# Windowed attention into a two-pass feed-forward: seven ff tiles in the first pass, a margin on what TensorE waits for, and the first keys ahead of other loads

## The chip, the cores and the metric

The kernel runs on one core of a Trainium2 chip. The metric is the device time of one execution in microseconds (us). Before the change three executions took 1095.8, 1096.32 and 1097.32 us, so the median is 1096.32. Engines are called as the profile calls them: PE is TensorE (PEld its weight loads), DVE is VectorE, ACT is ScalarE, POOL is GpSimd and SP is SyncE, which issues every DMA here.

## The reference

Batch 8, 8 heads, 576 positions, head size 64. Each position attends to itself and the 127 before it, with a slope per head; the result, 4608 tokens of 512, goes through a feed-forward with 2048 inner columns.

```python
scores = scale * np.matmul(q, k.transpose(0, 1, 3, 2))
bias = slopes[:, None, None] * (-np.abs(rel).astype(np.float32))[None, :, :]
mask = (rel >= 0) & (rel < window)          # window = 128
scores = np.where(mask, scores + bias[None], -1000000000.0)
attn = softmax(scores)
x = (attn @ v).transpose(0, 2, 1, 3).reshape(4608, 512)
h = x @ w_in                                # 512 x 2048
sp = np.maximum(h, 0.0) + np.log1p(np.exp(-np.abs(h)))
out = (h * erf(sp)) @ w_out                 # 2048 x 512
```

## The kernel before

**Attention.** Two heads make a pair, so there are 32 pairs. A pair is worked in two spans: the first has three query tiles of 128 (score tiles 0, 1, 2), the second has two (3 and 4), which makes 160 score tiles. A score tile is a product on PE (line 520 for the first 16 spans, in plain fp32; line 531 for the rest, with k split into a high and a low part), the bias and row minimum on DVE (line 542), the exponential on ACT (line 552) and the division by the row sum on POOL (line 577). Then PE transposes the probabilities (line 595), DVE or ACT copies them out, and PE multiplies them with v (line 613). The first 16 spans are the "early" ones: the first spans of pairs 0 to 7, then their second spans. An early span loads q into a tile `a`, which POOL scales by a power of two for each head (line 455, with the table `head` of line 376), and k into a pair of tiles `kz`, whose other half of partitions POOL has cleared once (line 368). There are two such pairs of `kz` tiles, used in turn, and four `a` tiles. Later pairs load raw q and k (`qr`, `kr`), and DVE, ACT and POOL split them (lines 472 to 490).

**Feed-forward.** The 4608 tokens are 12 chunks of 384, the 2048 inner columns are 16 tiles of 128 ("ff tiles"). A unit is one chunk with one ff tile: a first group of 12 products (line 795, tile `h`), softplus and erf on ACT, a product, a high and a low part on DVE, ACT or POOL, and a second group of 9 products (line 855, tiles `o`). The first pass runs NF1 ff tiles over all chunks among the attention's work, as the chunks of x come out of it, and stores its partial sums (`pd`); the second pass runs the remaining ff tiles and adds the partial sums. Each weight tile arrives as 64-bit floating point words and is taken apart into a high and a low part (lines 684 to 704: one operation on ACT, five on DVE, a copy on any of three engines, and a last subtraction on DVE that gives `wli` or `wlo`). The weights of the second pass take over the attention's memory (`FIT` of them in each of two rows, the others where first-pass weights stood), so they are prepared after the attention has ended.

**What sets the order.** Every operation is put into a plan with a cost per engine, its buffers and a time `at`; `Plan.run` then walks through simulated time and gives each engine, whenever it is free, the ready operation with the lowest `at`. An operation counts as ready when the last of its inputs has ended plus a hop between the two engines (`hop`, line 140). A transfer is taken to need its bytes at 360 GB/s, one after another on a single line (line 278), plus two fixed times. The order found in this way is written out: on the chip each engine works through its list in that order and waits at whatever is not ready. PE fills gaps that the plan sees with products of a zero tile (`warm`, 40 of them, line 399). `step_time` gives score tiles their `at` (TE apart for the first NE tiles, TA after that), and TM is the spacing of the first pass's units, chosen so that all of them together span the same planned time for any NF1.

Of the kernel before, what the change touches and what calls it, by code (L numbers as in the profile page):

```python
# [8 lines left out]
F32 = mybir.dt.float32  # L9
# [8 lines left out]
B, H, S, D = 8, 8, 576, 64  # L18
NPAIR = H // 2
P = 128  # L20
WIN = 128
DM = H * D
# [4 lines left out]
NTT = CH // P  # L27
LOG_EXP_SET = "natural_log_exp_and_others"

NF1 = 6  # L30
FIT = 8
UPR = (4, 4)
TAIL = (2, 2)
EARLY = 16
# [5 lines left out]
PB, XB, OB, TB, TBB = 8, 3, 3, 2, 2  # L40
BT = 0

TE, NE = 2.3, 28
TA = 1.8
LL, LP, LT = 15, 6, 0
TM = 1.2 * TA * 20 / (1.5 * NF1)
# [85 lines left out]
class Plan:  # L132
# [7 lines left out]
    def hop(self, src, dst):  # L140
        if src == "PE":
            return 0.0 if "PE" in dst else 0.2
        return 0.2 if "Pool" in dst else 0.14

    def __init__(self):
        self.ops = []
# [36 lines left out]
    def run(self):  # L183
# [6 lines left out]
        transfer = 0.0  # L190
# [48 lines left out]
        while events:  # L239
            t = heapq.heappop(events)  # L240
            while events and events[0] <= t:
                heapq.heappop(events)
            while done and done[0][0] <= t + 1e-9:
                _, _, o = heapq.heappop(done)
                for b in o.bufs:
                    b.users -= 1
                    if b.users == 0 and b.tag is not None:
                        empty[key(b)].append(b.slot)
                for x in o.outs:
                    x.left -= 1  # L250
                    if not x.left:
                        late = max(
                            d.end + d.lag + (self.hop(d.engine, x.costs))
                            for d in x.deps
                        )
                        enable(x, max(late, t))
            for e in ("SP", "PE", "Act", "DVE", "Pool"):
                while free.get(e, 0.0) <= t + 1e-9 and ready.get(e):
                    best = None
                    for o in ready[e]:  # L260
                        if o.ready > t + self.WAIT[e] + 1e-9 or (best and (best.at, best.seq) < (o.at, o.seq)):
                            continue
                        if fits(o) and all(t + o.costs[e] <= max(free[x], t) + c for x, c in o.costs.items()):
                            best = o
                    if best is None or best.ready > t + 1e-9:
                        break
                    for x in best.costs:
                        ready[x].remove(best)
                    for b in best.bufs:
                        if b.tag is not None and id(b) not in placed:  # L270
                            placed.add(id(b))
                            b.slot = empty[key(b)].pop(0)
                            head[key(b)] += 1
                    best.engine, best.start = e, t
                    best.end = on_pe(best, t) if e == "PE" else t + best.costs[e]
                    free[e] = best.end
                    if best.moved:
                        transfer = max(transfer, best.end + 0.65) + best.moved / 360e3
                        best.lag = transfer + 0.9 - best.end
                    order.append(best)  # L280
                    heapq.heappush(done, (best.end + best.lag, best.seq, best))
                    heapq.heappush(events, best.end)
                    heapq.heappush(events, best.end + best.lag)
# [33 lines left out]
def dma(nbytes, n=1, us=0.475):  # L317
    return dict(costs={"SP": n * us}, moved=nbytes)
# [23 lines left out]
class Attention:  # L342


    def __init__(self, tc, plan, ctx, actx, qT, kT, vb, bias, ident, moe):
        self.nc, self.plan = tc.nc, plan
        self.qT, self.kT, self.vb = qT, kT, vb
        self.bias, self.ident, self.moe, self.spare = bias, ident, moe, (moe.ps_h, moe.ps_o)
        sb = lambda name: actx.enter_context(tc.tile_pool(name=name, bufs=1))
        ps = lambda name: ctx.enter_context(tc.tile_pool(name=name, bufs=1, space=PSUM))  # L350
        self.raw, self.split, self.pp, self.ptp, self.xsb = (
            sb(n) for n in ("raw", "split", "pp", "ptp", "xsb")
        )
        self.ps = ps("ps_a")
        vpool = sb("vpool")
        self.vbd = []
        for i in range(2):
            t = vpool.tile([P, 9, P], F32, tag=f"vbd{i}", name=f"vbd{i}")
            v = Buf(shape=[P, 9, P], ap=t)
            plan.op({"Pool": 1.2}, lambda e, t=t: self.nc.gpsimd.memset(t, 0.0), w=[v], at=-1)  # L360
            self.vbd.append(v)

        self.plain = []
        for i in range(2):
            pair = [Buf(self.split, [P, S], F32, f"kh{j}", 2, f"kz{i}_{j}") for j in range(2)]
            for j, k in enumerate(pair):
                zero = slice((1 - j) * D, (2 - j) * D)
                plan.op({"Pool": 0.6}, lambda e, k=k, zero=zero: self.nc.gpsimd.memset(k[zero, :], 0.0),
                        w=[k], at=-3)
            self.plain.append(pair)  # L370
        self.head = Buf(self.split, [P, NPAIR], F32, "head", 1, "head")

        def powers(e):
            for g in range(NPAIR):
                for j in range(2):
                    self.nc.gpsimd.memset(self.head[j * D : (j + 1) * D, g : g + 1], 2.0 ** (2 * g + j))

        plan.op({"Pool": 0.8}, powers, w=[self.head], at=-3)
        self.order = [(b, g) for b in range(B) for g in range(NPAIR)]
        self.step = self.loads = 0  # L380
        self.seq = 0
        self.warm_up()

        for w in range(2):
            for i in range(2 * NPAIR):
                self.span(i, w, self.operands(i, w), self.values(i, 4 * w, 6 + 3 * w))
        for i in range(2 * NPAIR, len(self.order)):
            operands, v = self.operands(i), self.values(i, 0, 9)
            for w in range(2):
                self.span(i, w, operands, v)  # L390
# [11 lines left out]
    def operands(self, i, w=None):  # L402

        nc, op = self.nc, self.plan.op
        sync = nc.sync.dma_start
        b, g = self.order[i]
        at = step_time(self.step) - LL
        q0, q1 = (0, S) if w is None else SPANS[w][1:3]
        k0 = max(0, q0 - WIN)
        nq, nk = q1 - q0, q1 - k0  # L410
        early = self.seq < EARLY
        nm = f"{i}_{w}"
        n = self.seq
        self.seq += 1
        if early:
            q = Buf(self.split, [P, S], F32, f"a{n % 2}", 2, "a" + nm)
            k = self.plain[n % 2]

            def both(e):
                for j in range(2):  # L420
                    rows = slice(j * D, (j + 1) * D)
                    sync(k[j][rows, :nk], self.kT[b, g, rows, k0:q1])

            op(emit=both, w=k, at=at, **dma(P * nk * 4, 2))
        else:
            q = Buf(self.raw, [P, S], F32, "qr", 1, "qr" + nm)
            k = Buf(self.raw, [P, 2, S], F32, "kr", 1, "kr" + nm)
            src = self.kT[b, g, :, k0:q1].rearrange("(j d) s -> d j s", j=2)

            def both(e):  # L430
                for half in range(2):
                    sync(k[half * D : (half + 1) * D, :, :nk], src)

            op(emit=both, w=[k], at=at, **dma(2 * P * nk * 4, 2, 0.65))
        op(emit=lambda e: sync(q[:, :nq], self.qT[b, g, :, q0:q1]), w=[q], at=at, **dma(P * nq * 4))
        at = step_time(self.step) - LP
        return (*(self.early_parts if early else self.parts)(nm, g, q, k, nq, nk, at), q0, k0)
# [222 lines left out]
class Weights:  # L660

    def __init__(self, nc, plan, place, stage, w_in, w_out, ffs):
        self.nc, self.plan, self.place, self.stage = nc, plan, place, stage
        self.src = (w_in, w_out)
        self.ffs = list(ffs)
        self.t = {}

    def prepare(self, which, f, at, after=()):  # L670
        nc, op = self.nc, self.plan.op
        nm = f"{'io'[which]}{f}"
        raw = Buf(self.stage, [P, DM, 2], I32, "wr", 2, f"wr{nm}")
# [1 line left out]
        t = Buf(self.stage, [P, DM], I32, "wt", 2, f"wt{nm}")  # L675
        op(emit=lambda e: nc.sync.dma_start(
            raw.all.rearrange("p n two -> p (n two)"), self.src[which][f].bitcast(I32)),
            w=[raw], at=at - 20, **dma(P * DM * 8))

        words = lambda k: raw[:, :, k]  # L680
        flt = lambda x: x.all.bitcast(F32)
# [204 lines left out]
def tile_kernel(ctx, tc, qT, kT, vb, w_in, w_out, bias, out, nb=B):  # L886
    nc = tc.nc
# [17 lines left out]
    stage = ctx.enter_context(tc.tile_pool(name="stage", bufs=1))  # L905
    moe = Moe(tc, plan, ctx, x_dram, part, out)
    actx = ctx.enter_context(ExitStack())
    Attention(tc, plan, ctx, actx, qT, kT, vb, bias_sb, ident, moe)
    ops = list(plan.ops)


    n1 = nch * NF1
    t0 = LEAD
    t1 = t0 + n1 * TM
    w1 = Weights(nc, plan, lambda k, f: (w1p, f"{k}_{f}"), stage, w_in, w_out, range(NF1))
    for k in range(2):
        for f in range(NF1):
            w1.prepare(k, f, t0 - W1A + (f * W1C + W1B * k) * TM)
# [60 lines left out]
```

## Time and profile before

| what | value |
| --- | --- |
| median of three executions | 1096.32 us |
| the profiled execution, its own time | 1095.57 us |
| its span, first to last instruction | 1093.8 us |
| outside the span (difference) | 1.8 us |
| mean granted clock of TensorE | 0.994 |
| first product that counts (line 520) starts | 6.72 us |
| first unit of the feed-forward (line 795) starts | 50.2 us |
| last product of the attention (line 613) starts | 502.7 us |

The tables by stretch give, for each engine, the time in which it was busy and the number of its instructions; PEclk is the share of TensorE's full clock that was granted. A wait is put down to the instruction whose end released it. An fp32 product shows as two instructions, so 40 `warm` products are 80 in the trace.

### The profile page before, as it was taken

To read this page: it belongs to the slowest core of one execution; us is meant where nothing else is said; L and a number is where in the kernel's file an instruction comes from. 1 tells how busy PE (TensorE), PEld (TensorE's weight loads), DVE (VectorE), ACT (ScalarE), POOL (GpSimd) and SP (SyncE) were. 2 spreads that over 40 slices of the span, in tenths; PEclk is the share of its full clock that TensorE was granted. 3 is DMA by queue.
4 is the path that set the end of the run, shared out by engine and by line. 5 is a ranking of instruction groups with operands and counts; after the bars stand their busy time and mean duration, and the time that the engine had idled before them with its cause. 6 is when DMAs were issued, how large, how long until landed. Compare 5 with 4: busy or idle time off the path is not lost.

```text
span 1093.8 us, 16894 instructions
## 1 busy us (share of the span) xinstructions
PE 1065.1 (97%) x6000; PEld 975.3 (89%) x6000; DVE 677.9 (62%) x1531; ACT 676.2 (62%) x1393; POOL 289.6 (26%) x438
## 2 busy tenths in 40 slices
PE   7998999999999989999999999999999999999998
PEld 7987889988999989899999998999999999999996
DVE  2789999878887787764888873433333334343342
ACT  4766887776777677765766663645535545445461
POOL 5645657565545555441100000000000000000000
PEclk9998999999999999999999999999999999999999
DMA  6553644646453453412434411220210210202102
GB/s 177 148 157 111 179 132 122 197 110 173 132 138 106 130 157 98 134 34 88 135 117 131 149 61 46 87 63 24 87 58 29 87 54 34 87 19 68 58 17 71
DMA packets 88260, 109.51 MB, mean 100 GB/s; under 512 B 45808, under 2 KB 58224, under 8 KB 88176
## 3 DMA queue, kind: packets, MB, share of 16 engines
q1 hardware_dynamic: 88176, 108.42, 33.6%
q8 instruction: 48, 0.79, 0.3%
q14 instruction: 36, 0.29, 0.1%
HBM read 80.08 MB, written 28.31 MB: 99 GB/s over the span
## 4 chain that ended last, share of the span: by engine, by line
PE 86%; DVE 5%; DMA 3%; POOL 3%; issue 1%; SPq 0%; ACT 0%; POOLq 0%; DVEq 0%
PE o L855 34%; PE h L795 34%; PE px L613 7%; PE t L595 5%; PE s L531 4%; POOL p L577 3%; PE s L520 2%; DMA xr<-xd 1%; DVE p L542 1%; DVE a_None L489 1%; DMA a<-q_t 1%; DMA kz<-k_t 1%; DMA wri<-w_in 1%; DVE hs L836 1%; DVE kl_None L486 0%
## 5 line engine op out<-in xcount | busy, mean ns | idle before, releaser
L795 PE MATMUL h<-xh,whi 128*128 128x384 f32 x768 | 263.9, 344 | 0.7 <-DVE xh L781 0.5
L795 PE MATMUL h<-xh,wli 128*128 128x384 f32 x768 | 260.0, 339 | 0.5 <-DVE wli L704 0.5
L795 PE MATMUL h<-xl,whi 128*128 128x384 f32 x768 | 259.1, 337 | 0.9 <-DVE xl L770 0.9
L855 PE MATMUL o<-who,gh 128*128 128x512 f32 x576 | 228.1, 396 | 0.0
L855 PE MATMUL o<-who,gl 128*128 128x512 f32 x576 | 227.5, 395 | 0.0
L855 PE MATMUL o<-wlo,gh 128*128 128x512 f32 x576 | 227.1, 394 | 0.0
L577 POOL TENSOR_SCALAR p<-p,st 128x256 f32<-128x256 f32 (+2 forms) x320 | 197.3, 635 | 95.2 <-DVE st L570 94.2
L777 ACT COPY hs<-h 128x384 f32<-128x384 f32 x113 | 53.8, 477 | 233.7 <-PE h L795 233.2
L552 ACT ACTIVATE p<-p,st 128x256 f32<-128x256 f32 (+2 forms) x320 | 149.0, 468 | 33.4 <-DVE st L542 32.9
L781 DVE COPY hs<-h 128x384 f32<-128x384 f32 x79 | 43.8, 555 | 192.6 <-PE h L795 192.4
L795 PEld LDWEIGHTS h<-xh,whi 128*128 128x128 f32 x768 | 145.4, 189 | 8.6 <-DVE xh L781 0.9
L795 PEld LDWEIGHTS h<-xl,whi 128*128 128x128 f32 x768 | 145.3, 189 | 7.5 <-DVE xl L770 1.1
L795 PEld LDWEIGHTS h<-xh,wli 128*128 128x128 f32 x768 | 144.8, 189 | 1.0 <-DVE wli L704 1.0
L542 DVE CUSTOM_DVE_ANT_0 p<-s,bias_sb 128x256 f32<-128x256 f32 (+2 forms) x320 | 108.8, 378 | 40.4 <-PE s L531 16.1
L855 PEld LDWEIGHTS o<-who,gl 128*128 128x128 f32 x576 | 108.0, 188 | 23.3
L855 PEld LDWEIGHTS o<-wlo,gh 128*128 128x128 f32 x576 | 108.3, 188 | 16.1
L855 PEld LDWEIGHTS o<-who,gh 128*128 128x128 f32 x576 | 108.4, 188 | 15.4
L836 DVE TENSOR_TENSOR hs<-s,hs 128x768 f32<-128x768 f32 x96 | 90.9, 970 | 23.6 <-ACT s L826 23.5
L840 DVE TENSOR_TENSOR gl<-hs,gh 128x768 fp32r<-128x768 f32 x96 | 90.8, 963 | 0.7 <-ACT gh L777 0.6
L595 PE MATMUL t<-ident,p 128*128 128x128 f32 x544 | 82.1, 276 | 6.6 <-POOL p L577 6.2
L595 PEld LDWEIGHTS t<-ident,p 128*128 128x128 f32 x544 | 64.6, 143 | 17.1 <-POOL p L577 9.8
L826 ACT ACTIVATE s<-s 128x768 f32<-128x768 f32 x96 | 76.0, 839 | 0.6
(78 smaller groups left out, 1486.3 us busy)
## 6 DMA issues: line engine op xcount, KB each, us to landing
xr<-xd SPq DMA_DIRECT2D x22, 768.0 KB, 4.3
kr_None<-k_t SPq DMA_DIRECT2D x48, 288.0 KB, 4.3
pd<-ot SPq DMA_DIRECT2D x36, 256.0 KB, 3.6
ot<-pd SPq DMA_DIRECT2D x36, 256.0 KB, 3.0
wri<-w_in SPq DMA_DIRECT2D x16, 512.0 KB, 4.3
wro<-w_out SPq DMA_DIRECT2D x16, 512.0 KB, 3.7
out_dram<-ot SPq DMA_DIRECT2D x32, 256.0 KB, 2.1
qr_None<-q_t SPq DMA_DIRECT2D x24, 288.0 KB, 4.3
```

The costliest lines, as they stand in the source:

```text
L542: nc.vector.tensor_tensor_reduce(out=pt[:m, c0:c1, j, :], in0=blocks(ps[:m, j, :n]), in1=blocks(self.bias[:m, c0 * 64 : c1 * 64]), scale=- ...
L552: nc.scalar.activation(dst, dst, AF.Exp, bias=low[:m, j : j + 1], scale=-1.0, accum_out=total[:m, j : j + 1],)
L577: nc.gpsimd.tensor_scalar(dst, dst, totals[t][:m, j : j + 1], 1.0, op0=ALU.mult, op1=ALU.mult)
L595: nc.tensor.matmul(ps[:, col : col + P], lhsT=p[t][:, kb].rearrange("p j d -> p (j d)"), rhs=self.ident[:, :], is_transpose=True, start=no ...
L613: self.nc.tensor.matmul(dst[:, q0 - base : q1 - base], lhsT=v[:, blk], rhs=sb[sbi][:, off : off + q1 - q0], start=(blk == order[0][0]), st ...
L777: self.nc.scalar.copy(out, src)
L781: self.nc.vector.tensor_copy(out, src)
L795: nc.tensor.matmul(ps[:, :CH], lhsT=ww[:, cs], rhs=xx[:, k], start=(k2 + k + n == 0), stop=(k2 + k + n == 4),)
L826: A.activation(s[:, :n], s[:, :n], AF.Erf)
L836: op({"DVE": dve(n2)}, lambda e, s=s, hs=hs, n=n: V.tensor_tensor(hs[:, :n], s[:, :n], hs[:, :n], ALU.mult), r=[s, hs], w=[hs], at=at)
L840: op({"DVE": dve(n2)}, lambda e, gh=gh, gl=gl, hs=hs, n=n: V.tensor_tensor(gl[:, :n], hs[:, :n], gh[:, :n], SUB), r=[hs, gh], w=[gl], at=at)
L855: nc.tensor.matmul(po.all, lhsT=g[:, j, cs], rhs=w.all, start=(u["start"] and n == 0), stop=(u["end"] and n == 2),)
```

## The change

NF1 goes from 6 to 7 and FIT from 8 to 7: the first pass has 84 units instead of 72, the second 108 instead of 120. TM follows, so units of the first pass are planned closer together. TE goes from 2.3 to 2.0 (the first 28 score tiles are planned earlier). The planner's hop into a PE operation from any other engine, DMAs included, grows by 0.6 us, and its transfer rate falls from 360 to 250 GB/s; both only alter the order. There are four pairs of `kz` tiles instead of two (the new ones in buffers of the low k parts, `kl`), so POOL clears eight tiles. And the loads of raw k (`kr`) and of weights (`wri`) gain dependences on early k loads, so that a load of raw k waits for the early k load four before the latest one, and a first-pass weight load for the fourth k load.

```diff
-NF1 = 6
-FIT = 8
+NF1 = 7
+FIT = 7
...
-TE, NE = 2.3, 28
+TE, NE = 2.0, 28
...
-        return 0.2 if "Pool" in dst else 0.14
+        return 0.2 if "Pool" in dst else 0.14 + 0.6 * ("PE" in dst)
...
-                        transfer = max(transfer, best.end + 0.65) + best.moved / 360e3
+                        transfer = max(transfer, best.end + 0.65) + best.moved / 250e3
...
-        for i in range(2):
-            pair = [Buf(self.split, [P, S], F32, f"kh{j}", 2, f"kz{i}_{j}") for j in range(2)]
+        for i in range(4):
+            pair = [Buf(self.split, [P, S], F32, f"k{'hl'[i // 2]}{j}", 2, f"kz{i}_{j}") for j in range(2)]
...
+        self.loaded = []
...
-            k = self.plain[n % 2]
+            k = self.plain[n % 4]
...
             op(emit=both, w=k, at=at, **dma(P * nk * 4, 2))
+            self.loaded.append(Buf(ap=True))
+            self.loaded[-1].writer = self.plan.ops[-1]
...
-            op(emit=both, w=[k], at=at, **dma(2 * P * nk * 4, 2, 0.65))
+            op(emit=both, r=self.loaded[-4:-3], w=[k], at=at, **dma(2 * P * nk * 4, 2, 0.65))
...
-            w=[raw], at=at - 20, **dma(P * DM * 8))
+            r=self.later, w=[raw], at=at - 20, **dma(P * DM * 8))
...
-    w1 = Weights(nc, plan, lambda k, f: (w1p, f"{k}_{f}"), stage, w_in, w_out, range(NF1))
+    w1 = Weights(nc, plan, lambda k, f: (w1p, f"{k}_{f}"), stage, w_in, w_out, range(NF1), attention.loaded[3:4])
```

What this does to the order shows best at three places. The first is SP's list of transfers at the very start; in the names the number behind `a` or `kz` is the early span's or the tile pair's number, `vbd` is v, `wri` is a weight tile, `kr8` and `qr8` belong to the first later pair. Before:

```order
L422 DMA kz0_0_166<-k_t 64x384
L422 DMA kz0_1_172<-k_t 64x384
L435 DMA a3_0_186<-q_t 128x384
L422 DMA kz1_0_177<-k_t 64x384
L422 DMA kz1_1_183<-k_t 64x384
L676 DMA wri0_205<-w_in 128x1024
L676 DMA wri1_209<-w_in 128x1024
L448 DMA vbd0_160<-v_b 64x6x64 x2
L432 DMA kr8_None_230<-k_t 64x2x576 x2
L448 DMA vbd1_161<-v_b 64x6x64 x2
L422 DMA kz0_0_166<-k_t 64x384
L422 DMA kz0_1_172<-k_t 64x384
```

Now, at the same place of SP's list:

```order
L439 DMA a3_0_185<-q_t 128x384
L423 DMA kz1_0_176<-k_t 64x384
L423 DMA kz1_1_181<-k_t 64x384
L423 DMA kz2_0_187<-k_t 64x384
L423 DMA kz2_1_192<-k_t 64x384
L439 DMA qr8_None_205<-q_t 128x576
L423 DMA kz3_0_196<-k_t 64x384
L423 DMA kz3_1_201<-k_t 64x384
L452 DMA vbd0_160<-v_b 64x6x64 x2
L452 DMA vbd1_161<-v_b 64x6x64 x2
L681 DMA wri0_257<-w_in 128x1024
L439 DMA a4_0_263<-q_t 128x384
```

The third pair's k stood behind two weight tiles, v and raw k; now it follows the second pair's at once, in tiles of its own, and the weights come after v.

The second place is the start of POOL's list and of PE's list. On POOL `head` is the table of scales and `a0` the first q; before:

```order
L368 MEMSET kz0_0_166 64x576
L368 MEMSET kz0_1_172 64x576
L368 MEMSET kz1_0_177 64x576
L368 MEMSET kz1_1_183 64x576
L376 MEMSET head_188 64x1 x8
L360 MEMSET vbd0_160 128x1152
L455 TENSOR_SCALAR a0_0_162<-a0_0_162,head_188 128x384
```

Now four more clears stand ahead of the first scaling of q:

```order
L368 MEMSET kz1_1_181 64x576
L368 MEMSET kz2_0_187 64x576
L368 MEMSET kz2_1_192 64x576
L368 MEMSET kz3_0_196 64x576
L368 MEMSET kz3_1_201 64x576
L376 MEMSET head_207 64x1 x8
L360 MEMSET vbd0_160 128x1152
L459 TENSOR_SCALAR a0_0_162<-a0_0_162,head_207 128x384
```

Everything that POOL does at the start moves back by these four rows. On PE, `s3` are score tiles of the fourth pair and `t0` is the first transpose; before:

```order
L520 MATMUL s3_0_324<-kz1_0_177,a3_0_186 128x128
L520 MATMUL s3_0_324<-kz1_1_183,a3_0_186 128x128
L520 MATMUL s3_1_333<-kz1_0_177,a3_0_186 128x256
L520 MATMUL s3_1_333<-kz1_1_183,a3_0_186 128x256
L399 MATMUL warm_ps_168<-warm_164 128x128 x2
L595 MATMUL t0_0_0_343<-ident_62,p0_0_226 128x128
```

Now, at the same eleven score tiles into the program:

```order
L524 MATMUL s3_0_323<-kz3_0_196,a3_0_185 128x128
L524 MATMUL s3_0_323<-kz3_1_201,a3_0_185 128x128
L400 MATMUL warm_ps_174<-warm_164 128x128 x2
L524 MATMUL s3_1_332<-kz3_0_196,a3_0_185 128x256
L524 MATMUL s3_1_332<-kz3_1_201,a3_0_185 128x256
L400 MATMUL warm_ps_174<-warm_164 128x128 x14
L599 MATMUL t0_0_0_365<-ident_62,p0_0_244 128x128
```

Fourteen zero products now stand between the last of these score tiles and the first transpose. The twelve that stood between the second and the third pair's scores are gone from there, and 22 instead of 17 precede the first score.

The third place is DVE's list around pair 10 (score tiles 51 to 55), where the first pass's last weights are finished: `p10_0` is the pair's first score tile, `wlo5` and `wlo6` are the sixth and seventh weight tile of w_out. Before, the twelfth and last tile is done ahead of the pair's first score:

```order
L781 CAST who5_1928<-wto5_1844 128x512
L489 TENSOR_TENSOR a11_None_0_1896<-qr11_None_1813,a11_None_0_1896 64x576
L704 TENSOR_TENSOR wlo5_1946<-wto5_1844,who5_1928 128x512
L570 RECIPROCAL st9_1_1848<-st9_1_1848 128x4
L542 ISA p10_0_1958,st10_0_1959<-s10_0_1930,bias_sb_63 128x2x64
```

Now the fourteenth is done behind the pair's fourth score tile:

```order
L697 SCALAR_TENSOR_TENSOR wqo6_1975<-wro6_1774,wqo6_1975 128x512
L841 TENSOR_TENSOR hs8_1590<-s8_1898,hs8_1590 128x768
L705 TENSOR_TENSOR wto6_1995<-wto6_1995,wqo6_1975 128x512
L574 RECIPROCAL st10_0_1887<-st10_0_1887 128x6
L546 ISA p10_3_2061,st10_1_2062<-s10_3_2034,bias_sb_63 128x4x64
...
L709 TENSOR_TENSOR wlo6_2079<-wto6_1995,who6_2065 128x512
L845 TENSOR_TENSOR gl8_2088<-hs8_1590,gh8_2051 128x768
```

So DVE has two more weight tiles within about the same score tiles.

More of the change, by code (lines that the diff above doesn't have):

```diff
@@ L660, with __init__ @@
 class Weights:
-    def __init__(self, nc, plan, place, stage, w_in, w_out, ffs):
+    def __init__(self, nc, plan, place, stage, w_in, w_out, ffs, later=()):
         self.nc, self.plan, self.place, self.stage = nc, plan, place, stage
         self.src = (w_in, w_out)
+        self.later = later
         self.ffs = list(ffs)
@@ L907, in tile_kernel @@
     actx = ctx.enter_context(ExitStack())
-    Attention(tc, plan, ctx, actx, qT, kT, vb, bias_sb, ident, moe)
+    attention = Attention(tc, plan, ctx, actx, qT, kT, vb, bias_sb, ident, moe)
     ops = list(plan.ops)
```

## The prediction

> **What bounds the kernel now.** I read the page's totals first, then a table by stretch, PE's waits, and the timeline of the start.
>
> ```profile
> span 1093.8 us, 16894 instructions
> PE 1065.1 (97%) x6000; PEld 975.3 (89%) x6000; DVE 677.9 (62%) x1531; ACT 676.2 (62%) x1393; POOL 289.6 (26%) x438
> ```
>
> PE is busy 97% of the span, and the change removes no product: it only moves units between the passes. So the gain can come only from time in which PE stands still, works on zero products, or has half its clock. The profiled execution took 1095.57 us, 1.8 more than its span and 0.75 less than the median 1096.32; I add changes to the span and keep those two offsets.
>
> I cut the span where score tiles 1, 9, 25, 33, 49, 57 and 81 and the end of the attention's products stand (four score instructions a tile, counted along the timeline: the 96 up to 49.5 are 24 tiles).
>
> ```profile
> 6.70:49.50 42.80, 20.82 (x96) 16.50 (x97) 0.96 0.61 165
> ```
>
> ```profile
> core 0: us, PE busy (x) PEld busy (x) DVE busy (x) ACT busy (x) POOL busy (x), PEclk, DMA share, GB/s
> 0.00:6.70 6.70, 5.65 (x34) 5.65 (x35) 0.17 (x1) 1.28 (x1) 5.60 (x21) 1.00 0.63 177
> 6.70:21.30 14.60, 9.93 (x59) 9.00 (x58) 4.65 (x29) 6.76 (x30) 5.50 (x11) 0.90 0.86 222
> 21.30:49.50 28.20, 28.20 (x193) 26.82 (x192) 20.03 (x84) 19.37 (x72) 17.05 (x35) 0.99 0.49 135
> 49.50:80.50 31.00, 29.08 (x192) 27.42 (x191) 23.90 (x74) 19.86 (x67) 17.27 (x31) 1.00 0.59 157
> 80.50:147.30 66.80, 60.46 (x359) 54.78 (x357) 62.67 (x152) 51.74 (x117) 36.99 (x46) 0.95 0.46 135
> 147.30:171.60 24.30, 22.89 (x143) 20.74 (x142) 21.84 (x58) 20.86 (x56) 14.57 (x17) 1.00 0.59 157
> 171.60:241.70 70.10, 68.66 (x457) 63.79 (x456) 61.22 (x172) 50.92 (x153) 46.70 (x67) 1.00 0.49 138
> 241.70:502.70 261.00, 253.82 (x1644) 236.82 (x1641) 194.98 (x553) 186.59 (x508) 133.89 (x201) 0.99 0.44 122
> 502.70:1093.80 591.10, 586.44 (x2937) 530.29 (x2936) 288.49 (x412) 318.87 (x392) 11.97 (x12) 1.00 0.22 71
> ```
>
> Three regimes show. At the start PE waits for loads. From 80.5 to 147.3 DVE is busy 62.67 of 66.8 us (94%): there DVE sets the pace. After 171.6 PE has short waits on other engines until the attention ends; after 502.7 it has none but the 5 us of the last stores, so nothing is to be had there.
>
> ```profile
> PE t L595 <- POOL p L577: 6.2, 10, 1.3
> PE s L531 <- DVE st L542: 4.8, 2, 2.8
> PE s L520 <- DMA kz<-k_t: 4.7, 1, 4.7
> PE s L520 <- DVE st L542: 3.4, 3, 1.8
> ```
>
> The longest single wait, 4.7 us, is for the third pair's k; the others are for probabilities from POOL and score buffers from DVE.
>
> **The change part by part. The start.** These are rows of PE, SP, POOL and DVE there:
>
> ```profile
> 6.72 4.51 PE L520 MATMUL s<-kz,a 128*128 128x128 f32 x24
> 11.07 2.84 PE L399 MATMUL warm_ps<-warm 128*128 128x128 f32 x24
> 18.58 5.32 PE L520 MATMUL s<-kz,a 128*128 128x128 f32 x20 [4.67 <-DMA kz<-k_t]
> 24.18 1.26 PE L595 MATMUL t<-ident,p 128*128 128x128 f32 x10
> 11.90 3.33 SPq L422 DMA_DIRECT2D kz<-k_t  x2
> 1.36 2.40 POOL L368 MEMSET kz<- 64x576 f32 x4
> 5.81 0.60 POOL L455 TENSOR_SCALAR a<-a,head 128x384 f32<-128x384 f32 x1
> 12.24 2.53 POOL L577 TENSOR_SCALAR p<-p,st 128x128 f32<-128x128 f32 x6 [3.15 <-DVE st L570]
> 11.96 0.18 DVE L570 RECIPROCAL st<-st 128x6 f32<-128x6 f32 x1
> ```
>
> The third pair's k is issued at 11.90, behind 1 MB of weights, v and raw k, and PE takes it at 18.58: between 11.07 and 18.58 lie 7.5 us without useful work. With its own tiles and its place behind the second pair this load no longer ends last. What is late next is POOL: four more clears at 2.40/4 = 0.6 us move the first scaled q from 5.81 to 8.2, done at 8.8, so the first score starts at about 9.1 instead of 6.72, a loss of 2.4. Then DVE: it took six tiles 5.24 us after the first score (11.96 - 6.72), so at 14.3; two more of the third pair at about 0.7 each and a reciprocal bring 15.9, which frees the score buffer for the eleventh tile, on PE until 16.8. Then 14 zero products (28 instructions; 24 took 2.84) end at 20.1, and the first transpose follows, if POOL has divided the first pair: reciprocal at about 15, the scaling of `a4` (0.6) and 2.53 us give 18.2. That leaves 1.9 us for the load of `a4`, which now waits behind a weight tile on SP, and which POOL meets ahead of those divisions. So the transpose comes at 20.1 instead of 24.18, with the same eleven score tiles done: **-4**. Bounds: -7.5 if the whole hole closed, +2.4 if only POOL's clears told. I take the worked-out value, near the middle. Both lists then run on with PE full in the row 21.30:49.50. The first weight tile comes later than before, but ACT meets it only ahead of the copies behind that transpose, so a wait for it is hidden until 20.1.
>
> **The DVE stretch.** In both orders all first-pass weights are done by about score tile 57, but there are 14 instead of 12. One tile costs DVE the six rows
>
> ```profile
> L689 DVE SCALAR_TENSOR_TENSOR wto<-wqo,wto 128x512 int32<-128x512 int32 x5 | 4.1, 829 | 0.0
> L700 DVE TENSOR_TENSOR wto<-wto,wqo 128x512 f32<-128x512 f32 x5 | 3.9, 779 | 0.0
> L704 DVE TENSOR_TENSOR wlo<-wto,who 128x512 fp32r<-128x512 f32 x5 | 3.9, 777 | 0.3 <-POOL who L779 0.2
> L692 DVE SCALAR_TENSOR_TENSOR wqo<-wro,wqo 128x512 f32<-128x512 uint32 x5 | 3.8, 765 | 0.0
> L687 DVE TENSOR_SCALAR wto<-wqo 128x512 int32<-128x512 int32 x5 | 3.0, 592 | 0.0
> L691 DVE TENSOR_SCALAR wqo<-wto 128x512 int32<-128x512 int32 x5 | 2.8, 560 | 0.0
> ```
>
> or 4.3 us together, two tiles 8.6. Other work leaves DVE for ACT: DVE's list up to score tile 57, each row at its line's mean, grows by 4.4, of which 2.3 stand before tile 25, where DVE has room (rows 6.70 to 49.50: 24.68 of 42.8 busy). That leaves 2.1. PE is not the bound here, and what it does meanwhile is less: up to score tile 57 its list held 17 first and 8 second groups of units, now 16.5 and 6.7. The groups cost
>
> ```profile
> 512.08 2.10 PE h L795 x12
> 510.00 2.08 PE o L855 x9
> ```
>
> so 0.5 x 2.10 + 1.3 x 2.08 = 3.8 us of units are put off to where PE is the bound. The stretch costs **+5.9**. Bounds: 0 if the rest of DVE's idle time takes it in and PE meets no more waits; 8.6 + 3.8 = 12.4 if no work leaves DVE. I take the count, as the order shows what leaves.
>
> **After 171.6 us.** PE's idle time there is 70.10 - 68.66 and 261.00 - 253.82, together 8.6 us, and a clock of 0.99 costs up to 2.6. From score tile 57 to the last attention product PE now has 43.5 first and 45.6 second groups between the score tiles instead of 38 and 40.7: 5.5 x 2.10 + 4.9 x 2.08 = 21.7 us more to do while the others deliver. With the hop longer by 0.6 the planner also sets PE's readers later behind their writers. The upper bound of the gain is 21.7: the attention ends when it did, with all of this done beside it. The lower is 0: PE ends the attention 21.7 later and waits as before. I take the visible idle time and half of the clock's share: **-10**. Where the edit is free: the copying of chunks, softplus tables (three rounds more with a third table load) and partial sums run on ACT, busy 237.52 of 331.1 there; if that cover went, one round costs the load of a table.
>
> ```profile
> 171.60:502.70 331.10, 322.48 (x2097) 300.61 (x2096) 256.19 (x724) 237.52 (x660) 180.59 (x268) 0.99 0.45 126
> ```
>
> The second pass's weights come no later against PE: 24 first groups of the first pass stand behind the attention's last product instead of 17, and there are 18 tiles to prepare instead of 20.
>
> Would a margin of 0.6 do? Two late waits tell:
>
> ```profile
> 395.17 1.76 DVE L489 TENSOR_TENSOR a_None<-qr_None,a_None 64x576 fp32r<-64x576 f32 x1
> 383.91 0.75 DVE L489 TENSOR_TENSOR a_None<-qr_None,a_None 64x576 fp32r<-64x576 f32 x1
> 447.11 7.62 DMA xr<-xd
> ```
>
> The first ran 1.0 us over its usual 0.75 with POOL's divisions beside it, and PE stood 2.8 us; the second is a load whose 768 KB the planner put at 2.2 us of transfer (now 3.1) and which took 7.62 in all. Both exceed 0.6, so the margin alone wouldn't have covered them; the added units have to. [...]
>
> **Sum:** -4 + 5.9 - 10 = -8, a profiled run of 1087.5 and a median of **1088**.
>
> **Rivals.**
> - *The attention keeps its own pace.* The put-off units cost nothing since all later idle time takes them: -4 and about -15 after 171.6, near 1077. For it: from 241.70 to 502.70 no other engine is busy over 75%. Against: DVE is at 87% from 171.60 to 241.70, and the visible 8.6 is less than 15. It covers 1070 to 1082.
> - *Waits longer than the margin stay.* POOL and DVE deliver late by 1 us and more, as shown; the late gain is only what the start and the DVE stretch take back: -4 + 5.9 - 2 = 0, so 1096. The changed rates then reorder the lists and do nothing else.
> - *Slower: DVE is the bound up to the first pass's last weights.* All 8.6 us of the two tiles tell, 3.8 of units are put off, and PE, waiting more between 80 and 170, loses clock again as in the row 80.50:147.30 (0.05 of 66.8 is 3.3): -4 + 8.6 + 3.8 + 3.3 - 6 = +6, so 1102. It decides where the seventh `wlo` ends later than PE's list needs it, that is where DVE's share between score tiles 33 and 57 rises above 94%.
>
> **How the numbers follow.** My forecast (1082 to 1094) gets 0.47, the first rival 0.25, no change 0.13, slower 0.15. A measurement can tell 0.2%, 2.2 us, from no change. Faster is then 0.72, same 0.13, slower 0.15. The range of 8 in 10 reaches from the start and the late gain at 18 with nothing lost between, 1074, to 1100, inside the slower rival.
>
> **What would show it.** Right: the first score near 9.1, no wait for `kz` after it, the first transpose near 20; DVE over 90% busy between score tiles 33 and 57 with PE's clock below 1; PE's idle time behind score tile 57 under 4 us; the attention's last product near 509 (502.7 - 4 + 2.1 - 10, plus 21.7 - 3.8 of units done before it). Wrong: POOL waiting on `a4` ahead of its divisions beyond 18 us, a first unit later than 50 us, or PE waiting for second-pass weights behind the attention.

## The result and the profile after

| what | before | changed |
| --- | --- | --- |
| median, same chip, four executions each | 1096.82 us | 1084.67 us |
| ratio to before, 95% interval | 1 | 0.9882 [0.9866, 0.9897] |
| the profiled execution, its own time | 1095.57 us | 1082.40 us |
| span | 1093.8 us | 1080.6 us |
| PE not busy (span less PE's busy time) | 28.7 us | 17.3 us |
| first score starts | 6.72 us | 8.90 us |
| first unit of the feed-forward | 50.18 us | 47.52 us |
| last product of the attention | 502.69 us | 507.50 us |

The kernel became faster by 12 us, where 8 were forecast. (One execution each of e4, e6 and e10 below took 1757 to 6005 us and is left out; as it is the one that e4's profile shows, the same kernel was run again as e10.) The totals of the changed kernel's page show where to look:

```profile
span 1080.6 us, 16860 instructions
...
PE 1063.3 (98%) x6000; PEld 975.9 (90%) x6000; DVE 678.3 (63%) x1535; ACT 682.0 (63%) x1398; POOL 293.5 (27%) x436
```

PE's busy time fell by 1.8 us only (1065.1 to 1063.3); the time in which it was not busy fell by 11.4. The table by stretch says when. It is cut at score tiles 1, 25, 33, 57, 81 and the attention's last product, which now stand elsewhere; columns as in the prediction's table.

```profile
0.00:8.90 8.90, 7.51 (x44) 7.32 (x44) 0.17 (x1) 1.28 (x1) 7.65 (x25) 1.00 0.63 183
8.90:46.84 37.94, 37.55 (x252) 34.99 (x253) 28.50 (x120) 27.16 (x106) 24.86 (x47) 1.00 0.62 168
46.84:73.50 26.66, 26.21 (x173) 25.10 (x171) 23.37 (x70) 16.36 (x55) 16.85 (x29) 1.00 0.69 189
73.50:165.60 92.10, 82.94 (x493) 75.60 (x492) 84.71 (x214) 71.10 (x181) 52.73 (x64) 0.94 0.52 143
165.60:237.20 71.60, 70.65 (x462) 65.53 (x461) 61.88 (x173) 55.83 (x156) 46.05 (x66) 1.00 0.53 149
237.20:507.50 270.30, 269.91 (x1744) 253.61 (x1742) 198.70 (x560) 199.72 (x521) 134.29 (x200) 1.00 0.41 114
507.50:1080.60 573.10, 568.57 (x2844) 513.71 (x2843) 281.00 (x401) 310.58 (x380) 11.06 (x9) 1.00 0.22 73
```

From score tile 57 to the attention's end PE now stands still for 0.95 + 0.39 = 1.3 us, where it was 8.6. Between tiles 33 and 57 it still does for 9.2 us, at a clock of 0.94: more than half of the 17.3 us that are left is there. PE's waits, grouped by what they were for (total, number, longest), agree:

```profile
PE t L599 <- POOL p L581: 5.7, 4, 3.0
PE o L860 <- DVE wlo L709: 1.3, 2, 1.0
...
PE s L535 <- DVE st L546: 0.7, 2, 0.4
```

The wait of 4.7 us for the third pair's k is gone, and the score buffers (`st`) cost 0.7 instead of 4.8 and 3.4. The timeline of PE at the start:

```profile
1.05 7.51 PE L400 MATMUL warm_ps<-warm 128*128 128x128 f32 x44 [1.05 <-DVE warm L398]
8.90 5.06 PE L524 MATMUL s<-kz,a 128*128 128x128 f32 x28 [0.34 <-POOL a L459]
13.80 0.61 PE L400 MATMUL warm_ps<-warm 128*128 128x128 f32 x4
14.24 2.34 PE L524 MATMUL s<-kz,a 128*128 128x256 f32 x12
16.42 0.61 PE L400 MATMUL warm_ps<-warm 128*128 128x128 f32 x4
16.86 1.03 PE L524 MATMUL s<-kz,a 128*128 128x256 f32 x4
17.73 3.29 PE L400 MATMUL warm_ps<-warm 128*128 128x128 f32 x28
20.86 1.25 PE L599 MATMUL t<-ident,p 128*128 128x128 f32 x10
```

The first score waits for the q that POOL scales (8.90 instead of 6.72), eleven score tiles follow without a stop, and the first transpose comes at 20.86 instead of 24.18.

### The profile page after: what moved, and what is told of

It reads as the page before. It is cut to its first block, busy times and chain, and to the rows that moved or that the text cites. A ratio compares the mean times of both kernels' runs of the same rounds, so it can differ in the third digit from the quotient of the medians.

```text
span 1080.6 us, 16860 instructions
## 1 busy us (share of the span) xinstructions
PE 1063.3 (98%) x6000; PEld 975.9 (90%) x6000; DVE 678.3 (63%) x1535; ACT 682.0 (63%) x1398; POOL 293.5 (27%) x436
## 4 chain that ended last, share of the span: by engine, by line
PE 94%; POOL 3%; ACT 1%; DVE 1%; issue 1%; POOLq 0%
PE h L800 36%; PE o L860 36%; PE px L617 8%; PE t L599 6%; PE s L535 5%; PE s L524 2%; POOL p L581 1%; ACT p L556 0%; POOL kz L368 0%; PE warm_ps L400 0%; POOL kh_None L480 0%; ACT pa L499 0%; POOL a_None L480 0%; DVE p L546 0%; ACT s L829 0%
## 5 line engine op out<-in xcount | busy, mean ns | idle before, releaser
L581 POOL TENSOR_SCALAR p<-p,st 128x256 f32<-128x256 f32 (+2 forms) x320 | 201.4, 647 | 86.5 <-DVE st L574 83.1
L784 POOL TENSOR_SCALAR gh<-hs 128x768 fp32r<-128x768 f32 x18 | 20.8, 1157 | 375.5 <-DVE hs L841 375.4
L841 DVE TENSOR_TENSOR hs<-s,hs 128x768 f32<-128x768 f32 x96 | 89.7, 958 | 20.2 <-ACT s L831 20.2
L845 DVE TENSOR_TENSOR gl<-hs,gh 128x768 fp32r<-128x768 f32 x96 | 94.4, 1002 | 2.9 <-ACT gh L782 2.6
L599 PEld LDWEIGHTS t<-ident,p 128*128 128x128 f32 x544 | 65.8, 145 | 17.3 <-POOL p L581 7.0
```

What stands on the lines that cost most here:

```text
L581: nc.gpsimd.tensor_scalar(dst, dst, totals[t][:m, j : j + 1], 1.0, op0=ALU.mult, op1=ALU.mult)
L599: nc.tensor.matmul(ps[:, col : col + P], lhsT=p[t][:, kb].rearrange("p j d -> p (j d)"), rhs=self.ident[:, :], is_transpose=True, start=no ...
L841: op({"DVE": dve(n2)}, lambda e, s=s, hs=hs, n=n: V.tensor_tensor(hs[:, :n], s[:, :n], hs[:, :n], ALU.mult), r=[s, hs], w=[hs], at=at)
L845: op({"DVE": dve(n2)}, lambda e, gh=gh, gl=gl, hs=hs, n=n: V.tensor_tensor(gl[:, :n], hs[:, :n], gh[:, :n], SUB), r=[hs, gh], w=[gl], at=at)
```

## The experiments

Each kernel tries one part of the change alone, takes one out of the whole, or tests one of the reasons. In the table "hop" is the margin of 0.6 us on PE's dependences, "start" the four `kz` pairs with their dependences, "tile" NF1 7 with FIT 7. "Not busy" is the span less PE's busy time, from each page; "late" is the part of it between score tile 57 and the attention's last product. "Slack" is worked out from the traces: for every score tile that PE transposes between 170 and 505 us (100 to 110 in a kernel), the time from the end of POOL's last division to the first transpose that reads it; the table has its 10th percentile, and how many are under 0.2 us, where PE as good as waited.

| kernel | median, us | ratio [95%] | not busy, us | late, us | slack, us | under 0.2 us |
| --- | --- | --- | --- | --- | --- | --- |
| before | 1096.82 | 1 | 28.7 | 8.6 | 0.24 | 9 |
| before + start (e1) | 1095.85 | 0.9979 [0.9962, 0.9995] | 29.5 | 8.2 | 0.70 | 7 |
| before + tile (e2) | 1097.12 | 0.9987 [0.9974, 0.9999] | 26.9 | 3.6 | 0.17 | 12 |
| before + hop (e3) | 1097.93 | 1.0 [0.998, 1.0019] | 31.3 | 5.6 | 0.53 | 7 |
| before + start + hop (e9) | 1104.12 | 1.0056 [1.0038, 1.0074] | 35.9 | 5.5 | 0.90 | 4 |
| changed | 1084.67 | 0.9882 [0.9866, 0.9897] | 17.3 | 1.3 | 0.92 | 1 |
| changed, six tiles (e4, e10) | 1083.79, 1083.96 | 0.9863 [0.9836, 0.989], 0.9876 [0.9859, 0.9892] | 19.2 (e10) | 2.3 (e10) | 0.80 | 5 |
| changed, old rate of transfers (e5) | 1085.05 | 0.9881 [0.9866, 0.9896] | 20.2 | 4.3 | 1.10 | 4 |
| changed, old TE (e6) | 1084.73 | 0.9876 [0.986, 0.9893] | 20.1 | 2.1 | 0.85 | 5 |
| changed, old hop (e7) | 1098.0 | 0.9995 [0.9985, 1.0004] | 30.1 | 4.6 | 0.06 | 12 |
| changed, two `kz` pairs (e8) | 1088.13 | 0.9905 [0.989, 0.992] | 22.0 | 2.2 | 0.99 | 0 |
| changed, without sign step (e11) | 1083.0 | 0.9869 [0.9854, 0.9884] | 16.3 | 1.4 | 0.98 | 1 |
| changed, clears on DVE (e12) | 1088.27 | 0.9915 [0.9901, 0.993] | 22.5 | 2.2 | 0.62 | 5 |

Each ratio is to runs of the kernel before on the same chip (their medians were 1096.82 to 1098.64 us). The last four columns are of one execution each, those of e3 and e9 some 3 and 4 us above the median, so 1 or 2 us between them mean little. Late time and slack do not go together: e1 has a slack of 0.70 us with the old hop and stands nearly as long as the kernel before, and e2 has less slack than that kernel and stands for less than half as long.

**One part alone: the start (e1).**

```diff
-        for i in range(2):
+        for i in range(4):
...
-            k = self.plain[n % 2]
+            k = self.plain[n % 4]
```

with the dependences of the change.

> The kernel before with only the four pairs of kz tiles and the new dependences of raw-k and weight loads (six ff tiles, old hop, old transfer rate, old TE). Theory A (the start keeps its gain): the third pair's scores follow the second's without a wait, the first transpose comes near 20 us instead of 24, and the time falls by about 4: 1092 to 1094. Rival (given back): the DVE-bound stretch behind it takes the 4 us back, PE waits there longer, and the time stays at 1096 to 1098.

The first unit came at 47.16 us instead of 50.18, so the start does gain; but tile 57 came at 172.20 instead of 171.64. The waits of this kernel's PE show what took the 3 us back:

```profile
PE t L599 <- POOL p L581: 8.0, 8, 1.8
PE s L524 <- DVE st L546: 5.3, 1, 5.3
PE t L599 <- DVE pa L503: 3.8, 2, 3.5
```

Two long waits, of 5.3 and 3.5 us, for a score buffer and for copied probabilities. Alone, the start is worth 0.2%, 2 us.

**The tile alone (e2).**

```diff
-NF1 = 6
-FIT = 8
+NF1 = 7
+FIT = 7
```

> The kernel before with only NF1 = 7 and FIT = 7. Theory A (cover): the units added beside the attention take the late waits, idle time of PE behind score tile 57 falls from 8.6 us to under 3, about -10 there; two more weight tiles cost 1 to 6 before it: 1087 to 1092. Rival (margin): late waits are a matter of the planned order, not of cover; with the old hop they stay at 7 us or more, and the weight tiles cost: 1096 to 1103.

This is the table by stretch of that kernel from score tile 33 to 57, and from there to the attention's last product:

```profile
81.80:183.50 101.70, 89.40 (x518) 81.23 (x517) 89.02 (x222) 76.34 (x183) 50.17 (x60) 0.93 0.49 136
183.50:533.20 349.70, 346.13 (x2225) 322.29 (x2224) 262.33 (x728) 250.78 (x675) 191.32 (x276) 1.00 0.41 117
```

Later PE stands still for 3.6 us instead of 8.6, as added work should do; in the first row for 12.3, where the kernel before has 7.8 (91.1 less 83.35 between the same tiles). Cover late, paid for early: the sum is within 0.2% of nothing.

**The hop alone (e3).**

```diff
-        return 0.2 if "Pool" in dst else 0.14
+        return 0.2 if "Pool" in dst else 0.14 + 0.6 * ("PE" in dst)
```

> The kernel before with only the hop into PE longer by 0.6. Theory A (cover): late waits of 1 us and more exceed 0.6, most of the 8.6 us of idle time behind score tile 57 stays, and the time is 1093 to 1098. Rival (margin): the readers on PE stand later, the late idle time falls under 3 us, and the time is 1086 to 1090.

```profile
PE s L531 <- DVE st L542: 8.3, 10, 2.2
PE t L595 <- POOL p L577: 8.1, 8, 4.3
PE s L520 <- DMA kz<-k_t: 6.1, 1, 6.1
```

These are its PE's waits: the wait for the third pair's k grew from 4.7 to 6.1, the first unit came at 54.31, and score buffers cost 8.3. The late slack rose to 0.53 and PE's late standing time fell to 5.6 us, yet nothing was gained.

**The whole, without the hop (e7).** The same line as in e3, undone in the changed kernel.

> The changed kernel with the old hop into PE. Theory R: 1083 to 1088, as the hop alone changed nothing on the kernel before. Rival M (the hop works together with the true rate): the idle time behind score tile 57 comes back to 6 us or more, 1090 to 1096.

The whole gain is gone, with the tile, the rates and the start still in. PE's waits for probabilities, and the longest of them on PE's timeline:

```profile
PE t L599 <- POOL p L581: 18.3, 14, 8.1
```

```profile
96.98 1.33 PE L599 MATMUL t<-ident,p 128*128 128x128 f32 x5 [8.12 <-POOL p L581]
```

They cost 18.3 us in 14 places; with the hop it is 5.7 in 4. PE's list in this kernel puts more transposes right behind the divisions: 12 of 100 have under 0.2 us, the 10th percentile is 0.06 us. But the table of slack begins at 170 us, and most of the loss lies ahead of that, from tile 33 to 57 in the first of these rows (the second reaches to the attention's last product):

```profile
69.80:171.60 101.80, 83.49 (x504) 76.52 (x502) 91.27 (x225) 73.81 (x190) 54.16 (x65) 0.93 0.50 135
171.60:521.10 349.50, 344.87 (x2211) 320.61 (x2210) 263.51 (x735) 251.10 (x669) 179.29 (x262) 1.00 0.43 119
```

PE stands still there for 9.1 us more than in the changed kernel (101.80 less 83.49, against 9.2), and for 3.3 more after it. The longest stop, 8.1 us, is far above the margin of 0.6, so it is another order of all engines, with other late deliveries, and not 0.6 us here and there. That the whole loses its gain without the hop is shown; by what way the hop leads the planner to the better order is not.

**The whole, with six tiles (e4, e10).**

```diff
-NF1 = 7
-FIT = 7
+NF1 = 6
+FIT = 8
```

> The changed kernel with NF1 = 6 and FIT = 8 again. Theory A (cover): start gain stays (-4), late gain goes: 1091 to 1095. Rival (margin): hop and rate hold the late gain without the seventh tile: 1083 to 1087.

The time was 1083.79 us, the same as with seven tiles. The profile is read from e10.

> The changed kernel with six ff tiles in the first pass and FIT 8, as in e4, for a usable profile. Theory (the hop alone clears the late waits): time 1083 to 1086 again, idle time of PE from score tile 57 to the last attention product under 4 us although 21.7 us less of units lie there, last attention product near 485 to 495. Rival (the tile's cover clears the late waits, and what it costs in DVE's stretch happens to be as much): idle time there 7 us or more, and the stretch from score tile 33 to 57 shorter by over 5 us than the unit work moved out of it explains.

Its stretches, from tile 33 to 57, and from there to the last product of the attention:

```profile
73.50:158.80 85.30, 74.83 (x467) 68.19 (x467) 78.55 (x205) 67.76 (x174) 54.34 (x66) 0.98 0.52 141
158.80:477.20 318.40, 316.10 (x2071) 295.33 (x2069) 253.81 (x716) 238.87 (x665) 172.11 (x257) 1.00 0.46 131
```

Late, PE stands still for 2.3 us, against 1.3 with the tile and 8.6 before: most of those waits go without any added work. (The attention's last product came at 477, earlier than the 485 to 495 I had expected.) With the tile the first row is 92.1 instead of 85.3, 6.8 us more, of which 5.5 are PE's own work (the products that the order has between these tiles, at their usual durations): the tile costs 1.3 us there and saves about as much later.

**The rates (e5, e6).**

```diff
-                        transfer = max(transfer, best.end + 0.65) + best.moved / 250e3
+                        transfer = max(transfer, best.end + 0.65) + best.moved / 360e3
```

> The changed kernel with the planned transfer rate at 360 GB/s again. The seventh tile did nothing (1084.26 without it), and start, tile and hop alone did little. Theory R (the rate): the plan now knows how long loads take, so POOL, DVE and PE no longer stand before late q, k and x; undone, most of the gain goes: 1092 to 1097. Rival T (TE or the parts together): 1084 to 1087 here, and the loss shows in the two next runs.

```diff
-TE, NE = 2.0, 28
+TE, NE = 2.3, 28
```

> The changed kernel with TE = 2.3 again. Theory R: TE only moves some units around the first 28 score tiles, 1083 to 1087. Rival T: early score tiles planned later let weight tiles and units in ahead of them, the stretch up to score tile 57 gets longer, 1090 to 1096.

1085.05 and 1084.73, with ratios that overlap the changed kernel's throughout: neither is needed for the time when all else is there.

**The start, undone (e8).** Two `kz` pairs in turn, without the added dependences.

> The changed kernel with two pairs of kz tiles and without the new dependences, so the third pair's k stands behind weights again. If the start's 4 us are kept to the end: 1088 to 1090, with a wait of 3 to 5 us for kz. If the DVE-bound stretch behind it gives them back: 1084 to 1086.

1088.13, with a ratio 0.0023 above the changed kernel's: the start is worth about 2.5 us in the whole by the ratios (3.5 by the medians, which are of two chips; the intervals just overlap), and about as much alone (e1). The wait is the one seen before the change, in this kernel's list of waits:

```profile
PE s L524 <- DMA kz<-k_t: 3.5, 2, 3.0
```

**Start and hop together (e9).** The diffs of e1 and e3 on the kernel before.

> The kernel before with two parts of the change only: the four kz pairs with their dependences, and the longer hop (six ff tiles, the old rates of transfers and of score tiles). Theory now (the hop sets the order in which PE's waits for POOL and DVE go away, and the start is kept only with it; the tile and the rates add nothing): 1084 to 1088, ratio 0.988 to 0.992, first score near 9, PE's idle time from score tile 57 to the attention's last product under 5 us. Rival (the late gain also needs the seventh tile or the new rates, as e2 showed a late gain from the tile alone): 1091 to 1096, with 6 us or more of idle time there.

Both theories missed: it is slower than before. The first score (8.90) and the late slack (0.90) are those of the changed kernel, but PE stands for 5.5 us late, and its timeline has two new long stops:

```profile
91.58 2.04 PE L524 MATMUL s<-kz,a 128*128 128x256 f32 x4 [5.62 <-issue]
...
657.84 0.79 PE L860 MATMUL o<-who,gh 128*128 128x512 f32 x1 [6.75 <-POOL who L784]
```

The first is in the stretch of the weights, with no releaser that the profile shows; the second is for a weight tile of the second pass, long after the attention, where neither the kernel before nor the changed one waits. So the margin is not enough. My reading, which no run isolates, is that the planner, which is greedy, also has to place DVE's and POOL's work well, and that whether it does shifts with every number it is given.

**Is DVE the bound (e11)?** This kernel leaves out DVE's step that puts the sign on the first pass's weights; the lists are otherwise those of the changed kernel.

```diff
-            (False, t, lambda: V.scalar_tensor_tensor(
+            (False, t, lambda: f < NF1 or V.scalar_tensor_tensor(
```

> The changed kernel with DVE's sign step (the scalar_tensor_tensor that puts the sign bit on the high part) left out for the 14 weight tiles of the first pass; it leaves out the signs of these weights, and nothing moves in any engine's list otherwise. That is 14 x 0.83 = 11.6 us less on DVE, about two thirds of it between score tiles 33 and 57. Theory (DVE bounds that stretch in the changed kernel): the stretch gets 5 to 8 us shorter, the time 1077 to 1080. Rival (the stretch is set by the chain score, DVE, ACT, POOL, transpose in the written order, and DVE's 92% is only where the room was used): 1083 to 1085, the stretch shorter by under 2 us.

DVE's busy time fell from 678.3 to 668.6 us. Its page, and the row from tile 33 to 57:

```profile
PE 1064.8 (99%) x6000; PEld 977.9 (90%) x6000; DVE 668.6 (62%) x1521; ACT 682.2 (63%) x1398; POOL 287.2 (27%) x436
```

```profile
73.50:165.90 92.40, 83.99 (x491) 77.20 (x491) 78.67 (x205) 71.07 (x181) 48.86 (x63) 0.93 0.52 141
```

6.0 us less on DVE in the stretch (84.71 to 78.67), and the stretch is 92.4 instead of 92.1. The order of every engine is otherwise unchanged, so DVE at 92% did not set the pace there. PE does stand for 0.8 us less (8.4 after 9.2), which a clock of 0.93 instead of 0.94 took back: the clock may hide about 1 us, not the 5 to 8 of the theory. The median is 1.7 us below the changed kernel's, less than the two intervals can tell apart.

**A better start (e12)?** POOL's four added clears were to go to DVE.

```diff
-                plan.op({"Pool": 0.6}, lambda e, k=k, zero=zero: self.nc.gpsimd.memset(k[zero, :], 0.0),
-                        w=[k], at=-3)
+                plan.op({"Pool": 0.6} if i < 2 else {"DVE": 0.6}, lambda e, k=k, zero=zero: (
+                        self.nc.vector if e == "DVE" else self.nc.gpsimd).memset(k[zero, :], 0.0), w=[k], at=-3 if i < 2 else -1.5)
```

> The changed kernel with the clears of the third and fourth kz pairs on DVE instead of POOL. DVE has nothing to do before 6 us, so POOL scales the first q 2.4 us sooner and the first score starts near 6.7 instead of 8.9. If the start is set by that score: first transpose 1.5 to 2.4 us sooner and the time 1082 to 1083. Rival (the first transpose waits for the division on POOL, behind the load of a4, which comes no sooner): first transpose within 0.7 us of 20.9 and the time 1084 to 1085.5.

PE's timeline shows the first score 2.4 us and the first transpose 2.0 us sooner, and what became of it:

```profile
6.47 5.06 PE L524 MATMUL s<-kz,a 128*128 128x128 f32 x28 [0.92 <-POOL a L459]
...
18.91 1.25 PE L599 MATMUL t<-ident,p 128*128 128x128 f32 x10
20.00 1.50 PE L400 MATMUL warm_ps<-warm 128*128 128x128 f32 x12
...
47.49 0.53 PE L800 MATMUL h<-xh,whi 128*128 128x384 f32 x1
```

Zero products fill the time won, the first unit comes at 47.49 instead of 47.52, and the order that follows is worse: from tile 33 to 57 it takes 95.5 us instead of 92.1, and PE stands still for 13.1 of them instead of 9.2. The time is 1088.27, beyond both expectations. So moving two pairs of clears to an engine that was idle (DVE is busy for 0.17 of the first 8.90 us in the changed kernel) lost 3.6 us through the order behind them. No version was found that beats the changed kernel by more than the intervals.

## Why the prediction was right, and where it was not

The sum was -8 us, the measured medians differ by -12.2 and the profiled spans by -13.2. I split the 13.2 as the prediction did, counting the units that are put off at the prices given there.

| step | predicted, us | measured, us | from |
| --- | --- | --- | --- |
| the start | -4 | -3.3 | first transpose 24.18 to 20.86 |
| the DVE stretch | +5.9 | +1.1 | tile 57 at 171.64 to 165.59 is -6.05; with 3.8 of units not yet done -2.2, less the start's -3.3 |
| tile 57 to the attention's end | -10 | -10.8 | 331.05 to 341.91 us with 21.7 of units more |
| after it | 0 | -0.1 | 591.10 to 573.12 us with 17.9 of units less |

**The start** went as worked out: first score at 8.90 (9.1 forecast), no wait for `kz` after it, DVE and POOL in time. The transpose came 0.8 us later than the 20.1 forecast, mostly because I counted 28 zero products' instructions ahead of it and left out the eight that stand between the scores (two rows of 0.61 us). Of the 3.3 us, e8 and e1 show some 2 to 3.5 in the end.

**The DVE stretch** is the term that was mis-sized, by 4.8 us. The prediction said "there DVE sets the pace" and priced two weight tiles by DVE's list, giving the hop no effect there. DVE is 92% busy and the clock 0.94, as foretold, but e11 shows for the changed kernel that taking DVE's work away does not shorten the stretch. What PE waits for there are mostly single late deliveries of probabilities (5.1 of the 9.2 us, in three places). Here e7 loses most: without the hop tiles 25 to 57 take 127.0 us (44.59 to 171.60), with it 118.8 (46.84 to 165.59), where the prediction gave the hop no effect at all. The tile's own price there, by e10, is 1.3 us, not 5.9. The rival that was slower hung on DVE's share rising above 94%; by e11 that share does not bound the stretch in the changed kernel.

**After 171.6 us** the size was right and the reason was not, so that -10.8 came so near to -10 was in part luck. The step that failed is the second half of "the margin alone wouldn't have covered them; the added units have to". The first half stands: with the margin alone (e3) PE's late standing time is 5.6 us, and with the start beside it (e9) 5.5. But with six tiles, and so without added units (e10), it is 2.3 us and the whole gain is there; without the hop but with the units (e7) it is 4.6 (349.5 less 344.87) and there is no gain. The units do cover something (e2: 3.6 instead of 8.6), but cost as much between tiles 33 and 57. The two late deliveries that I argued from were the largest, and few; small slack is common: before, 9 of 110 score tiles were transposed within 0.2 us of their division. In the whole the hop raises the 10th percentile of the slack from 0.06 (e7) to 0.92 us. That this is what clears the late waits is not shown, as e1 and e9 have nearly as much slack and keep 8.2 and 5.5 us of standing time.

**After the attention** nothing changed, as forecast; e9 shows that this was no matter of course.

**The rivals.** No change ("waits longer than the margin stay") is out: from 165.6 us on PE's waits for POOL and DVE are 0.6 and 0.7 us in all. The first rival (1077) had the late idle time right, which vanished, but not the price of the stretch between tiles 33 and 57, which is still there.

**What stays open.** The gain needs the hop (e7), but the hop alone gives nothing and with the start it loses (e3, e9). Whether any margin would do, or this one happened to lead the greedy planner to a good order, could only be told by runs with other margins, and none was made; e12 shows that the move of four clears can change the order for the worse by 3.6 us. Tile, rate of transfers and TE can each be undone at no cost (e4, e5, e6), so any two of them are enough beside start and hop, while start and hop without all three lose some 19 us against the changed kernel (e9). One of the three alone wasn't tried, so whether they matter by what they do, or only by moving the planner to another order, is not settled. Nor is it shown what makes the division late in the stretch up to tile 57: it is not the amount of DVE's work, and the rows below point to POOL and DVE together and to the place in DVE's list of the reciprocal that the division waits for.

## What to carry to other kernels

When an order is written out by a planner, cut the trace into stretches and ask in each where the bounding engine stands still and for what. A margin on that engine was worth about 12 us in the whole here (ratio 0.9995 without it, 0.9882 with it) and nothing by itself, and taking out any other single part cost 3.5 at most. The slack between each delivery and its reader is worth a look, but it did not foretell the time: e9 has as much as the changed kernel and is 19 us slower. Test a part by taking it out of the whole as well as by adding it alone: hop, tile and start alone gave 0 to 0.2%, and start with hop was slower than before. DVE's busy share of 92% did not make it the bound; taking work off it (e11: 6.0 us less, and the stretch 92.4 instead of 92.1) did tell.

## What the runs showed of the hardware

A stop of PE of 2.95 us came with half its clock for 6.8 us, longer than the stop lasted. These are the changed kernel's stretches of 2 us around that stop, its longest (89.3 to 92.25):

```profile
88.00:90.00 2.00, 1.30 (x8) 0.97 (x6) 2.00 (x4) 2.00 (x10) 2.00 (x3) 1.00 0.34 127
90.00:92.00 2.00, 0.00 (x0) 0.00 (x0) 2.00 (x5) 0.31 (x1) 2.00 (x3) 0.83 0.00 0
92.00:94.00 2.00, 1.33 (x5) 0.93 (x5) 2.00 (x3) 0.38 (x1) 2.00 (x3) 0.50 0.45 86
94.00:96.00 2.00, 1.85 (x8) 1.85 (x9) 2.00 (x4) 0.99 (x3) 2.00 (x3) 0.50 0.46 176
96.00:98.00 2.00, 2.00 (x12) 2.00 (x12) 1.79 (x6) 0.32 (x1) 0.77 (x3) 0.50 0.67 174
98.00:100.00 2.00, 2.00 (x14) 1.89 (x13) 0.50 (x2) 1.57 (x6) 0.71 (x1) 0.97 1.02 233
```

A clock of 0.83 over 90 to 92 means that it fell to 0.50 at about 91.3, some 2 us after PE had stopped. It was full again at 98.13, and of these 6.8 us PE was busy for 5.31 at half clock. The five transposes that follow the stop took 1.33 us there; five in the second row below, at full clock, took 0.77. Half of the 5.31 us, about 2.7 us of work by this estimate, was lost, nearly as much as by the stop itself. The length of one stop did not decide it, though. These are a second stop of the changed kernel, and the one that e10 (six tiles) has in place of the first:

```profile
128.09 0.44 PE L599 MATMUL t<-ident,p 128*128 128x128 f32 x2 [1.65 <-POOL p L581]
```

```profile
91.93 0.77 PE L599 MATMUL t<-ident,p 128*128 128x128 f32 x5 [1.61 <-POOL p L581]
```

They are equally long, but after the first the clock was 0.50 from 128.85 to 132.26, and after the second it stayed at 1.00 (the stretch from tile 33 to 57 has 0.98 with six tiles instead of 0.94). In the traces of the changed kernel and of the one before the clock is at 0.50 for 3.41 us (from 128.85; before, from 18.45 and 458.77) or for 6.83 (from 91.31; before, from 93.54); a last piece of each trace is cut off by its end. In the 3.41 us just ahead of 91.31 and of 128.85 PE was busy for 1.41 and 1.29 us; in the 3.41 us ahead of e10's 91.92, where the clock did not fall, for 1.81. So half clock came here after pieces in which PE was busy for 41% and 38% of the time, and not after one with 53%. That the share tells, and not one long stop, is my reading of these three; no run isolates it.

POOL's divisions took about twice as long (0.99 against 0.48 us in the changed kernel, see below) beside those operations of DVE that read two tensors, TENSOR_TENSOR and SCALAR_TENSOR_TENSOR in the trace. The same form, four at a time, on POOL in e7:

```profile
79.74 2.85 POOL L581 TENSOR_SCALAR p<-p,st 128x256 f32<-128x256 f32 x4 [3.96 <-DVE st L574]
...
91.81 5.11 POOL L581 TENSOR_SCALAR p<-p,st 128x256 f32<-128x256 f32 x4 [1.93 <-DVE st L574]
```

0.71 us each in the first row, beside two such operations of DVE, 1.28 in the second, beside six, and PE's stop of 8.1 us ends with that second row. Of the changed kernel's 192 divisions of this form the 103 that met none took 0.48 us in the median, and the 59 that ran beside one for over 0.4 us took 0.99 (worked out from the trace). e11 takes 14 such operations away, and POOL's busy time from tile 33 to 57 falls from 52.73 to 48.86 us. Why the divisions take longer then is not shown by any run.
